# A gated attention and SwiGLU kernel: five instead of six work pairs at the head of a run, and a place for VectorE's small steps before the products

## The chip, the cores and the metric

The kernel runs on one core of a Trainium2 chip. The metric is the time of one execution on the device in microseconds; several executions are timed, and their median is given. A smaller number is better. A profile of one more execution shows what each engine did: TensorE (PE; its weight loads are listed apart as PEld), VectorE (DVE), ScalarE (ACT), GpSimd (POOL), and the DMA queue of SyncE (SP).

## The reference

With S = 2048 rows, D = 512 and F = 1792, one input x goes through two branches, which a gate mixes row by row:

```python
g = sigmoid((x * gate_w).sum(-1, keepdims=True))
qkv = x @ wqkv                          # 32 heads of 16
p = softmax(q @ k.T * 16 ** -0.5)       # per head, 2048 x 2048
a = concat(p @ v) @ wo
b = (silu(x @ w1) * (x @ w3)) @ w2
out = g * a + (1 - g) * b
```

## The kernel before

Attention's scores are taken two heads at a time. Queries come in halves of 1024, so there are 2 halves x 16 pairs of heads = 32 steps, and a step has 16 blocks of 128 keys x 2 groups of 512 queries = 32 units; 1024 units in all. A unit is one **score**, `score` (L882): two matmuls (L888), one for each head of the pair, into one of two score buffers `S` in PSUM, and one exponential by ScalarE over 128 x 1024 (L892) into a buffer p (or v). Because there are two buffers `S`, a score needs the exponential of the score before the last to be over. The **product with V**, `pv` (L871), takes two units at a time and adds into the one bank `acc` (L875); after the last key block `evac` (L853) copies `acc` out (L857) and stores it.

All other matmuls, that is the projections of v, q and k that are still missing, the gate and up projections of the second branch, its second projection, and the output projection, are cut into blocks of 9 to 14 matmul pairs, which `blocks` (L767) lists in a fixed order. `feed` (L823) issues one **work pair**: one matmul on the upper 64 rows of the array and one on the lower 64, of two different blocks. When a block is through on one half, VectorE writes a small `tick` (L847), and the block goes on in the other half of the array; when it is through on both, its `done` is called, which empties the bank with VectorE. Three banks `f` serve the blocks; a bank or a second half is taken up again only some slots later (REST, GAP), so that VectorE has time.

The order of all of it is a string written out by hand, one letter for each action: Q is a score, F is a work pair, P is a product of two units. `run(n)` is a run of n scores: two scores, then work pairs, then a score and three work pairs repeated, a last score, and n/2 products. A double period `two` has eight scores and 15 work pairs, and its products in two groups. The string first has 4 runs of eight, then 15 times a run of twelve and two of ten ("thirds", 32 scores), then the LONG runs of eight, then the SHORT double periods.

A loop walks through the string. At each score it also issues what has come due: the loads of the next step's q and k (`load_step`, at a fixed score of each step), the splits of new weights on GpSimd, and the **small steps** of VectorE. These belong to the gate projection: when a gate block is done, its exponential (L494) is put into `soon` and issued behind the last score ahead of the products, and ten steps go into `small`: one addition (L495), eight reciprocals of 64 columns each (L497), and the multiplication by the up projection (L515) with the store of the result. One step is issued at a score, two where more than six are waiting. Once the last up block is done, `hurry` is set; from then on up to three steps are issued at a score.

Of the kernel before, what the change touches and what calls it, by code (L numbers as in the profile page):

```python
# [17 lines left out]
P = 128  # L18
S = 2048
D = 512  # L20
F = 1792
# [13 lines left out]
def gated_mix_kernel(ctx: ExitStack, tc: tile.TileContext, x, wqkv, wo, w1, w3, w2, gate_w, out):  # L35
# [272 lines left out]
    def load_step(s):  # L308
        half, j = divmod(s, NPAIR)
        load_q(j, half, s % 2)  # L310
        load_k(j, s % 2)
        load_guard(j, half, s % 2)
# [124 lines left out]
    small = nc.values_load(flag, min_val=0, max_val=1)  # L437
# [15 lines left out]
    soon, later, small, stages, loads = [], [], [], [], []  # L453
    hurry = False
# [186 lines left out]
    def divide(k, half):  # L641

        yield from reciprocals(k, half)
        for b in (2 * half, 2 * half + 1):
            for _ in range(5):
                yield
            if half == 0 and k < 3:
                o, r = slot("hx", F32), slot("gw", F32)
            else:
                both = wvp.tile([P, 2, 512], F32, name="v2")  # L650
                o, r = both[:, 0, :], both[:, 1, :]
            fetch_o(k, b, o, r)
            for _ in range(7):
                yield
            nc.gpsimd.tensor_mul(o, o, r)
            for _ in range(3):
                yield
            nc.sync.dma_start(N_d[P * k:P * k + P, 512 * b:512 * b + 512], o)
            yield
# [71 lines left out]
    def six_heads():  # L731

        k, rr = ND - 1, slice(0, 6 * DH)
        rows = lambda d: d[8 * k:8 * k + 6, 1024:2048].rearrange("h (a t) -> h a t", a=16)
        nc.sync.dma_start(dd[rr], rows(D_d))
        for _ in range(5):
            yield
        nc.vector.reciprocal(dd[rr], dd[rr])
        yield
        nc.sync.dma_start(rows(R_d), dd[rr])  # L740
        both = wvp.tile([P, 2, 512], F32, name="v2")
        pairs = [(both[:, 0, :], both[:, 1, :]), (slot("fr", F32), slot("sg", F32))]
        for b in (2, 3):
            o, r = pairs[b - 2]
            nc.sync.dma_start(o[rr], O_d[P * k:P * k + 6 * DH, 512 * b:512 * b + 512])
            src = R_d[8 * k:8 * k + 6, 512 * b:512 * b + 512]
            nc.sync.dma_start(r[rr], bass.AP(tensor=src.tensor, offset=src.offset, ap=[[S, 6], [0, DH], [1, 512]]))
        for _ in range(6):
            yield
        for b in (2, 3):  # L750
            o, r = pairs[b - 2]
            nc.gpsimd.tensor_mul(o[rr], o[rr], r[rr])
            split(Oh[k][rr, b - 2, :], Ol[k][rr, b - 2, :], o[rr])
            yield
# [68 lines left out]
    def feed(rest=REST, gap=GAP):  # L823
        nonlocal fed
        fed += 1
        did = 0
        for lane in range(2):
            if lanes[lane] is None:
                lanes[lane] = pick(lane, rest, gap)
        for lane in range(2):  # L830
            t = lanes[lane]
            if t is None:
                continue
            product, done, length = t["block"]
            did += 1
            second = t["turn"] is not None
            ins = product(t["ps"], slice(64 * lane, 64 * lane + 64), t["n"], second)
            if second and t["n"] == 0:
                after(ins, t["turn"])
            t["n"] += 1  # L840
            if t["n"] == length:
                lanes[lane] = None
                if second or t["alone"]:
                    done(t["ps"])
                    over[t["id"]] = clock
                else:
                    turn = nc.vector.memset(tick[:, 0:1], 0.0)  # L847
                    after(turn, ins)
                    t.update(n=0, turn=turn, since=clock)
                    ready[1 - lane].append(t)  # L850
        return did

    def evac(j, half):  # L853
        if half == 1 and j == NPAIR - 1:
            return
        u = wk.tile([P, 512], F32, name="u")
        nc.vector.tensor_copy(u, acc)  # L857
        for gq in range(2):
            t = 1024 * half + 512 * gq
            for h in range(2):  # L860
                r = 32 * (2 * gq + h)
                hh = 2 * j + h
                nc.sync.dma_start(D_d[hh:hh + 1, t:t + 512], u[r + DH:r + DH + 1, :])
        for gq in range(2):
            t = 1024 * half + 512 * gq
            for h in range(2):
                r = 32 * (2 * gq + h)
                hh = 2 * j + h
                nc.sync.dma_start(O_d[DH * hh:DH * hh + DH, t:t + 512], u[r:r + DH, :])

    def pv(two):  # L871
        for j, half, k, gq, n, p in two:
            for h in range(2):
                r = 32 * (2 * gq + h)
                nc.tensor.matmul(acc[r:r + DH + 1, :], V[:, k, 2 * j + h, :], p[:, h, :],  # L875
                                 start=k == 0, stop=k == NT - 1)
            if type(n) is int or issued < 32 * THIRDS:
                free.append(n)
        if k == NT - 1:
            evac(j, half)  # L880

    def score(j, half, k, gq):  # L882
        i = (NPAIR * half + j) % 2
        ps = psum2()
        t = 512 * gq
        for h in range(2):
            r = 64 * h
            nc.tensor.matmul(ps[:, h, :], Kt[i][r:r + 50, P * k:P * k + P],  # L888
                             Qt[i][r:r + 50, t:t + 512], start=True, stop=True)
        n = free.pop(0)  # L890
        p = (wk if type(n) is int else wvp).tile([P, 2, 512], F32, name=f"p{n}" if type(n) is int else n)
        nc.scalar.activation(p, ps, AF.Exp, scale=SCALE)  # L892
        return j, half, k, gq, n, p
# [3 lines left out]


    NP = 8
    THIRDS, LONG, SHORT = 16, 35, 28  # L900
    run = lambda n, m=6: "QQ" + "F" * m + "QFFF" * (n - 3) + "Q" + "P" * (n // 2)
    two = "QFFF" * 5 + "QPPQQPP"
    order = run(8) * 4 + (run(12) + run(10) * 2) * (THIRDS - 1) + run(8) * LONG + "QQ" + "F" * 7 + two * SHORT + "QFFF" * 5 + "QPPPP"
    MORE = ["v0", "v1", "v2", "v3"]
    free = list(range(NP))

# [2 lines left out]
    for i, c in enumerate(order):  # L909
        clock += 1 if c != "P" else 4  # L910
        if c == "Q":
            step = issued // 32 + 1
            if issued % 32 == (22 if 128 <= issued < 160 else 14 if issued < 640 else 21 if issued < 672 else 6) and step < 2 * NPAIR:
                assert NQK - qk_left >= (NQK if step >= NPAIR else 8 * min(step // 4, ND - 1))
                load_step(step)
            pend.append(score(*next(units)))
            issued += 1
            while splits and splits[0][0] <= issued:
                splits.pop(0)[1]()
            while soon and order[i + 1] == "P":  # L920
                soon.pop(0)()
            if issued % 128 == (40 if issued // 128 == 5 else 12) and 1 <= issued // 128 < 8:
                stages.append(divide((issued // 128 - 1) % 4, (issued // 128 - 1) // 4))
            if issued == 64 * NPAIR - 22:
                stages.append(six_heads())
            if small or later and hurry:
                for _ in range(3 if hurry else 1 + (len(small) > (6 if len(over) < FIRST - 16 else 0))):
                    if small or later and hurry:
                        (small or later).pop(0)()
            if loads and (hurry or issued % 2 or len(over) > FIRST - 12):  # L930
                loads.pop(0)()
            for stage in stages[:1]:
                if next(stage, stages) is stages:
                    stages.pop(0)
        elif c == "F":
            feed()
        else:
            pv(pend[:2])
            pend = pend[2:]
            if issued == 32 and not pend:  # L940
                free += MORE
# [92 lines left out]
```

## Time and profile before

| | before |
|---|---|
| median of 3 runs | 1396.81 us (1395.8 to 1397.53) |
| profiled execution, its own time | 1396.22 us |
| its span, first to last instruction | 1394.4 us |
| TensorE busy | 1386.5 us (99%) |
| ScalarE busy | 1025.1 us (74%) |
| VectorE busy | 491.5 us (35%) |
| GpSimd busy | 335.8 us (24%) |
| granted TensorE clock | 1.0 |

A row of the timeline gives the start in us from the span's start, the length in us, the engine, the line of the kernel, the operation, the tiles out<-in, the shape, and how many instructions are merged (x). In square brackets stands how long the engine stood idle before it, and what released it. A score is two matmuls on different rows of the array, which start together; so are the two of a work pair. A row of the waits has the waiting engine, tile and line, what it waited for, and then the sum in us, the number of waits and the longest. In the costliest groups of the page stand busy us, mean ns of one, and after the second bar the idle time before them with its releaser.

### The profile page before, as it was taken

How to read it: one execution, taken by the hardware profiler on the slowest of the kernel's cores; microseconds unless marked ns; L12 is line 12 of the kernel's file. 1: busy time of each engine (PE TensorE's matmuls, PEld its weight loads, DVE VectorE, ACT ScalarE, POOL GpSimd, SP SyncE). 2: the span in 40 equal slices, each digit the busy share in tenths (PEclk: the TensorE clock that was granted, in tenths of full speed). 3: DMA queues.
4: the chain of work that ended last, by engine and by line, in shares of the span. 5: the costliest groups of instructions: out<-in, count | busy, mean ns of one | idle time of the engine just before them, and what ended most of it. 6: DMA issues, size and time to landing. Idle time of an engine off the chain costs nothing.

```text
span 1394.4 us, 29335 instructions
## 1 busy us (share of the span) xinstructions
PE 1386.5 (99%) x11601; PEld 836.8 (60%) x11601; DVE 491.5 (35%) x1101; ACT 1025.1 (74%) x1151; POOL 335.8 (24%) x371
## 2 busy tenths in 40 slices
PE   9999999999999999999999999999999999999998
PEld 8766565656566565656565566566566555555554
DVE  6411111446464646564555545431111110110113
ACT  5467677777778677778777777777677787887884
POOL 6104344210111011101110114543253431232402
PEclk9999999999999999999999999999999999999999
DMA  9505455532323233332233424536534554444632
GB/s 272 139 10 144 98 145 142 120 94 62 77 71 91 60 80 78 76 86 71 62 78 77 107 67 108 122 107 124 110 105 91 118 123 88 96 100 98 162 110 84
DMA packets 111186, 141.30 MB, mean 101 GB/s; under 512 B 16422, under 2 KB 69414, under 8 KB 108066
## 3 DMA queue, kind: packets, MB, share of 16 engines
q1 hardware_dynamic: 109888, 137.40, 40.7%
q8 instruction: 93, 1.52, 0.5%
q10 hardware_dynamic: 1154, 1.97, 0.4%
q14 instruction: 51, 0.42, 0.1%
HBM read 90.69 MB, written 48.61 MB: 100 GB/s over the span
## 4 chain that ended last, share of the span: by engine, by line
PE 95%; DVE 1%; issue 0%; DVEq 0%
PE acc L875 33%; PE f L460 27%; PE S L888 19%; PE f L584 11%; PE f L674 2%; PE f L760 1%; PE f L681 1%; DVE xH L686 0%; DVE xL L686 0%; PE f L960 0%; DVE sg L497 0%; PE S L960 0%; DVE u L949 0%; DVE sg L515 0%; PE S L971 0%
## 5 line engine op out<-in xcount | busy, mean ns | idle before, releaser
L892 ACT ACTIVATE p<-S 128x1024 f32<-128x1024 f32 x864 | 817.2, 1027 | 273.6 <-PE S L888 272.2
L888 PE MATMUL S<-Qt,Kt 50*128 50x512 f32 x2048 | 409.9, 407 | 1.2 <-SPq L316 1.1
L875 PE MATMUL acc<-p,V 128*17 128x512 f32 x3456 | 400.8, 594 | 0.0
L888 PEld LDWEIGHTS S<-Qt,Kt 50*128 50x128 f32 x2048 | 187.8, 184 | 153.7 <-issue 73.0
L875 PEld LDWEIGHTS acc<-p,V 128*17 128x17 f32 x3456 | 88.7, 97 | 235.8 <-issue 235.1
L497 DVE RECIPROCAL sg<-sg 128x64 f32<-128x64 f32 x448 | 209.6, 518 | 52.6 <-issue 48.6
L460 PE MATMUL f<-xH,fl 64*128 64x512 f32 x1104 | 223.8, 394 | 0.1
L460 PE MATMUL f<-xH,fh 64*128 64x512 f32 x1104 | 221.6, 389 | 0.0
L460 PE MATMUL f<-xL,fh 64*128 64x512 f32 x1104 | 221.2, 389 | 0.0
L892 ACT ACTIVATE v<-S 128x1024 f32<-128x1024 f32 x160 | 153.0, 1027 | 54.7 <-PE S L888 54.4
L460 PEld LDWEIGHTS f<-xH,fh 64*128 64x128 f32 x1104 | 108.6, 184 | 23.3 <-DVE tick L847 0.2
L460 PEld LDWEIGHTS f<-xL,fh 64*128 64x128 f32 x1104 | 109.1, 187 | 22.4
L351 POOL CAST fh<-fr 128x512 fp32r<-128x512 f32 x35 | 22.1, 631 | 416.7 <-DMA fr<-in_B_w_dram 368.1
L460 PEld LDWEIGHTS f<-xH,fl 64*128 64x128 f32 x1104 | 108.8, 186 | 22.2 <-DVE raw L511 0.5
L847 DVE MEMSET tick<- 1x1 f32 x205 | 12.1, 59 | 310.4 <-PE f L584 152.5
L875 PE MATMUL acc<-v,V 128*17 128x512 f32 x640 | 77.1, 593 | 0.0
L584 PE MATMUL f<-xL,fh 64*128 64x512 f32 x208 | 66.2, 390 | 0.0
L584 PE MATMUL f<-xH,fl 64*128 64x512 f32 x208 | 65.9, 390 | 0.0
L584 PE MATMUL f<-xH,fh 64*128 64x512 f32 x208 | 61.2, 390 | 0.0
L857 DVE COPY u<-acc 128x512 f32<-128x512 f32 x31 | 21.5, 692 | 102.3 <-PE acc L875 102.3
L489 DVE COPY gs<-f 128x512 f32<-128x512 f32 x56 | 38.4, 687 | 53.2 <-PE f L460 52.4
L495 DVE TENSOR_SCALAR sg<-sg 128x512 f32<-128x512 f32 x56 | 26.1, 466 | 88.1 <-ACT sg L494 84.8
(221 smaller groups left out, 1417.2 us busy)
## 6 DMA issues: line engine op xcount, KB each, us to landing
Kt<-kH_d SPq DMA_DIRECT2D x124, 128.0 KB
h_d<-sg SPq DMA_DIRECT2D x56, 256.0 KB
sg<-h_d SPq DMA_DIRECT2D x43, 256.0 KB
fr<-in_B_w_dram SPq DMA_DIRECT2D x42, 256.0 KB
Qt<-qH_d SPq DMA_DIRECT2D x128, 64.0 KB
Kt<-kL_d SPq DMA_DIRECT2D x62, 128.0 KB
Qt<-qL_d SPq DMA_DIRECT2D x64, 64.0 KB
b_d<-yy SPq DMA_DIRECT2D x16, 256.0 KB
```

Of the source, the lines that this page charges most:

```text
L351: nc.gpsimd.tensor_copy(hi, src)
L460: return nc.tensor.matmul(ps, w[i == 1][r, k, :], (xL if i == 2 else xH)[b][r, k, :], start=n == 0 and not second, stop=n == 3 * ND - 1 an ...
L489: nc.vector.tensor_copy(gs, ps)
L495: small.append(lambda: nc.vector.tensor_scalar(sg, sg, 1.0, None, op0=OP.add))
L497: small.append(lambda q=q: nc.vector.reciprocal(sg[:, q:q + 64], sg[:, q:q + 64]))
L584: ins = nc.tensor.matmul(ps, hs[t][q][i == 1][r, P * o:P * o + P], (w2L if i == 2 else w2H)[q][r, o, :], start=n == 0 and not second, stop ...
L674: return nc.tensor.matmul(ps, ot[t][i == 1][r, P * k:P * k + P], wo_[k][i == 2][r, :], start=n == 0 and not second, stop=n == 3 * ND - 1 a ...
L681: return nc.tensor.matmul(ps, o_rows(t, k, i == 1)[r, :], wo_[k][i == 2][r, :], start=n == 0 and not second, stop=n == LATE - 1 and (secon ...
L857: nc.vector.tensor_copy(u, acc)
L875: nc.tensor.matmul(acc[r:r + DH + 1, :], V[:, k, 2 * j + h, :], p[:, h, :], start=k == 0, stop=k == NT - 1)
L888: nc.tensor.matmul(ps[:, h, :], Kt[i][r:r + 50, P * k:P * k + P], Qt[i][r:r + 50, t:t + 512], start=True, stop=True)
L892: nc.scalar.activation(p, ps, AF.Exp, scale=SCALE)
```

## The change

At the head of a run, behind its first two scores, stand five work pairs instead of six; only the four runs at the very beginning keep six. The string has 51 instead of 35 runs of eight behind the thirds, and 12 instead of 28 double periods. Beside that, ahead of the first product of each group, up to two of VectorE's waiting small steps are issued, as long as `hurry` is not set.

```diff
     NP = 8
-    THIRDS, LONG, SHORT = 16, 35, 28
-    run = lambda n, m=6: "QQ" + "F" * m + "QFFF" * (n - 3) + "Q" + "P" * (n // 2)
+    THIRDS, LONG, SHORT = 16, 51, 12
+    run = lambda n, m=5: "QQ" + "F" * m + "QFFF" * (n - 3) + "Q" + "P" * (n // 2)
     two = "QFFF" * 5 + "QPPQQPP"
-    order = run(8) * 4 + (run(12) + run(10) * 2) * (THIRDS - 1) + run(8) * LONG + "QQ" + "F" * 7 + two * SHORT + "QFFF" * 5 + "QPPPP"
+    order = run(8, 6) * 4 + (run(12) + run(10) * 2) * (THIRDS - 1) + run(8) * LONG + "QQ" + "F" * 7 + two * SHORT + "QFFF" * 5 + "QPPPP"
...
         elif c == "F":
             feed()
         else:
+            if order[i - 1] != "P" and not hurry:
+                for _ in range(2):
+                    if small:
+                        small.pop(0)()
             pv(pend[:2])
             pend = pend[2:]
```

## The prediction, made before the changed kernel ran

> **What bounds the kernel now.** I read the page first, then the order of time around one run in the middle, then the waits of the weight loads, then the first and last starts of each kind of period.
>
> ```profile
> span 1394.4 us, 29335 instructions
> PE 1386.5 (99%) x11601; PEld 836.8 (60%) x11601; DVE 491.5 (35%) x1101; ACT 1025.1 (74%) x1151; POOL 335.8 (24%) x371
> PE 95%; DVE 1%; issue 0%; DVEq 0%
> L892 ACT ACTIVATE p<-S 128x1024 f32<-128x1024 f32 x864 | 817.2, 1027 | 273.6 <-PE S L888 272.2
> ```
>
> TensorE is busy 99% of the span and is 95% of the chain that ended last, so the time is what the order string asks of TensorE, plus what TensorE waits. The share hides the second part: a busy matmul may be one that waits. ScalarE's exponentials are the candidate, because inside a run they follow each other without a gap. The timeline of one run of eight scores (the first row holds its first two scores; columns: start, length, engine, line, operation):
>
> ```profile
> 801.24 0.74 PE L888 MATMUL S<-Qt,Kt 50*128 50x512 f32 x4
> 801.84 1.03 ACT L892 ACTIVATE p<-S 128x1024 f32<-128x1024 f32 x1 [2.32 <-PE S L888]
> 802.98 0.19 PEld L888 LDWEIGHTS S<-Qt,Kt 50*128 50x128 f32 x2
> 803.20 0.40 PE L888 MATMUL S<-Qt,Kt 50*128 50x512 f32 x2
> 803.44 0.40 PE L460 MATMUL f<-xH,fl 64*128 64x512 f32 x2
> 807.84 0.39 PE L888 MATMUL S<-Qt,Kt 50*128 50x512 f32 x2
> 808.16 0.62 PE L875 MATMUL acc<-p,V 128*17 128x512 f32 x4
> 811.72 0.73 PE L888 MATMUL S<-Qt,Kt 50*128 50x512 f32 x4
> ```
>
> The period is 811.72 − 801.24 = 10.48 us. From the third score (803.20) to the eighth (807.84) stand five groups of a score and three work pairs, 20 slots in 4.64 us: **0.232 us a slot**. The third score reuses the buffer of the first, whose exponential ends at 801.84 + 1.03 = 802.87. The score's weight load starts 0.11 us after that, its matmul 0.33 us after. That is the margin the change spends.
>
> **What the exchange is worth without waits.** Both order strings count to 1024 scores, 2566 work pairs (F) and 512 products with V. 16 double periods become 16 more runs of eight; 45 runs of ten and twelve and 51 runs of eight carry one pair fewer than they would under the old rule, 96 in all, which pays for the 16 × 6 pairs by which an old run exceeds a double period. The starts of the regions:
>
> ```profile
> 102.54 0.73 PE L888 MATMUL S<-Qt,Kt 50*128 50x512 f32 x4
> 144.83 0.73 PE L888 MATMUL S<-Qt,Kt 50*128 50x512 f32 x4
> 738.08 0.74 PE L888 MATMUL S<-Qt,Kt 50*128 50x512 f32 x4
> 1095.40 0.73 PE L888 MATMUL S<-Qt,Kt 50*128 50x512 f32 x4
> 1114.87 0.73 PE L888 MATMUL S<-Qt,Kt 50*128 50x512 f32 x4
> 1359.68 0.73 PE L888 MATMUL S<-Qt,Kt 50*128 50x512 f32 x4
> ```
>
> 26 double periods take 1359.68 − 1114.87, 9.416 each. A run of eight costs 10.48 − 9.416 = 1.064 more for six pairs more, which at 0.232 are 1.39: a double period loses 0.33 us more at its extra switch between scores and products. Exchange: 16 × 1.064 = +17.0. Pairs left out: 96 × 0.232 = −22.3. Sum **−5.3 us**, if every pair left out shortens its run by a whole slot.
>
> **Does it? The third score then waits.** With five pairs the third score is wanted at 803.20 − 0.23 = 802.97, 0.10 us after the first exponential's end, and its weight load would start 0.12 us before that end. The trace has this situation where ScalarE was once late by itself:
>
> ```profile
> 642.78 1.03 ACT L892 ACTIVATE p<-S 128x1024 f32<-128x1024 f32 x1 [0.20 <-ACT v L892]
> 643.63 0.40 PE L460 MATMUL f<-xH,fh 64*128 64x512 f32 x2
> 643.86 0.19 PEld L888 LDWEIGHTS S<-Qt,Kt 50*128 50x128 f32 x2 [0.26 <-ACT p L892]
> 643.87 0.49 PE L888 MATMUL S<-Qt,Kt 50*128 50x512 f32 x2
> 644.20 0.39 PE L460 MATMUL f<-xH,fl 64*128 64x512 f32 x2
> 644.78 0.19 PEld L888 LDWEIGHTS S<-Qt,Kt 50*128 50x128 f32 x2 [0.16 <-ACT p L892]
> 648.97 0.62 PE L875 MATMUL acc<-v,V 128*17 128x512 f32 x4
> PEld S L888 <- ACT p L892: 49.8, 65, 0.9
> ```
>
> The exponential ends at 643.81; it is the weight load, not the matmul, that waits for it, and it starts 0.05 us later. The score's matmul is recorded at 643.87 but lasts 0.49 instead of 0.39, so it really began 0.10 later; its next pair at 644.20 says the same: 644.20 − 0.23 = 643.97, **0.16 us after the exponential's end**. That pair follows the last one by 644.20 − 643.63 = 0.57, against 0.46 for two slots. The waits view counts 65 such waits. So the new third score comes at 0.16 instead of 0.10: a stall of 0.05 to 0.06 a run. I take 0.055 (bounds 0.03 and 0.08, the rows being rounded to 0.01): 96 × 0.055 = **+5.3 us**, all of the gain.
>
> In the first run of each 32 scores the first exponential starts later:
>
> ```profile
> 780.01 0.73 PE L888 MATMUL S<-Qt,Kt 50*128 50x512 f32 x4
> 780.64 1.03 ACT L892 ACTIVATE p<-S 128x1024 f32<-128x1024 f32 x1 [2.45 <-PE S L888]
> ```
>
> 0.63 after the score against 0.60: 0.03 more in 15 runs of twelve and a fourth of 51, 28 runs: **+0.8**.
>
> **The pace behind it.** From then on each score's weight load waits, as at 644.78. From the pair behind that first late score to the products it takes 648.97 − 644.20 = 4.77, against 808.16 − 803.44 = 4.72 in the free run, over the same six scores: up to +0.05. A shorter stretch of the kind:
>
> ```profile
> 795.40 0.19 PEld L888 LDWEIGHTS S<-Qt,Kt 50*128 50x128 f32 x2 [0.27 <-ACT p L892]
> 795.73 0.39 PE L460 MATMUL f<-xH,fl 64*128 64x512 f32 x2
> 797.68 3.20 PE L875 MATMUL acc<-p,V 128*17 128x512 f32 x28
> ```
>
> 1.95 from the pair behind a late score to the products, two scores between; in the free run 4.72 less three groups of 0.928 is 1.94, so +0.01. I take 0.03 for a run of eight, 0.04 for ten, 0.05 for twelve, as the gaps are five, seven and nine: 51 × 0.03 + 30 × 0.04 + 15 × 0.05 = **+3.5** (bounds 0 and 6).
>
> **VectorE's small steps.** Excess over the plain periods: (1095.40 − 738.08) − 34 × 10.48 = 1.0 in the long runs; 738.08 − 102.54 = 635.5 against 15 × (144.83 − 102.54) = 634.4, 1.2 in the thirds. 2.2 us in all is what late VectorE work and late ScalarE starts cost there today. An example of the former:
>
> ```profile
> 486.21 0.39 PE L888 MATMUL S<-Qt,Kt 50*128 50x512 f32 x2
> 486.54 1.43 DVE L497 RECIPROCAL sg<-sg 128x64 f32<-128x64 f32 x3
> 487.44 0.06 DVE L847 MEMSET tick<- 1x1 f32 x1
> 487.49 0.40 PE L888 MATMUL S<-Qt,Kt 50*128 50x512 f32 x2
> 788.84 0.43 DVE L495 TENSOR_SCALAR sg<-sg 128x512 f32<-128x512 f32 x1 [2.02 <-ACT sg L494]
> 789.29 1.79 DVE L497 RECIPROCAL sg<-sg 128x64 f32<-128x64 f32 x4
> ACT p L892 <- ACT p L892: 0.7, 4, 0.2
> ```
>
> Reciprocals stand in front of what the next pair waits for, and the score comes after 1.28 instead of 0.93. The added pops take up to two of the ten steps of a gate block out of that stretch and put them before the products, where VectorE waits anyway. The late ScalarE starts (four at 0.2 in the last row, two or so more in the runs that write other buffers, as the one at 642.78) cost 0.10 each today (0.57 against 0.46 above), 0.6 in all; of the 1.6 left I credit VectorE's relief with half, **−0.8** (bounds −1.6 and +1.6, as the pattern of pairs against runs shifts). What the new place adds: the first popped step can wait for the gate's exponential, and the copy of the sums and the next ticks queue behind it; the run that began at 780.01 ends a period later, near 790.5, so that wait ended 1.7 us before the next run, and the copy behind it cannot start before the last product anyway: nothing, while the exponential comes no later than that. The late ScalarE starts meet no margin any more and cost all of their 0.2: six times 0.10, **+0.6**.
>
> **What moves beside it.** The gate blocks end, by the letters, after 668 scores instead of 643, so the loads for the second projection move past the request for step 21 (after 661 scores) and before that for step 22 (after 678).
>
> ```profile
> 921.08 12.31 SPq L546 DMA_DIRECT2D sg<-h_d  x6
> 933.96 0.42 SPq L300 DMA_DIRECT2D Qt<-qH_d  x1
> ```
>
> Today step 21's loads stand behind a block of 12.3 us; step 22's would then, and it is wanted 26 scores or some 34 us later. Nothing, unless the block grows to 34 us; then a wait of PE for Qt shows.
>
> **Sum**: −5.3 + 5.3 + 0.8 + 3.5 − 0.8 + 0.6 = +4.1. The profiled execution took 1396.2 us (span 1394.4, 1.8 around it), 0.6 under the median of the three. 1396.2 + 4.1 gives **1400.3**. Own range: stalls ±2.4, pace −3.5 to +2.5, VectorE −0.8 to +2.4; taken together 1396 to 1405.
>
> **Rivals.**
> 1. *The wait doesn't reach the third score* (the other side, faster). If the load of the weights may wait elsewhere and only the matmul needs the exponential, the gate lies at 0.05 after its end and the score is wanted at 0.10: no stall, no slower pace. −5.3 − 0.8 = −6: 1390. It decides at 0.10 us. Against it: the load itself waits at 643.86 and 644.78. In part (half the stall, no loss of pace) 1393. Chance 0.17. The Trainium skill, "TensorE: Matmul & The Clock Gate", the table at its head, says that TensorE's queue pulls weight loads ahead of matmuls in flight; by that rule alone the load would be out of the way and the time 1390, but a load that waits for a semaphore is not covered by it, and the 65 waits above speak against it.
> 2. *Stall as worked out, pace kept, VectorE relieved*: −5.3 + 5.3 + 0.8 − 0.8 = 0, 1396 to 1399. For it: the +0.01 over two scores. Chance 0.30.
> 3. *The stall is larger than the analog shows*: the left-out pair saves nothing, since the scores' pace is the exponentials' pace. +17: 1413; with a stall of 0.12 instead of 0.055, 1406. Against it: the pair at 644.20 stood 0.16 behind the exponential's end less one slot, after a longer wait than the one expected here. Chance 0.08.
> 4. My sum: 0.45.
>
> 0.2% of the median is 2.8 us, about what a measurement here can tell: 1394.0 to 1399.6 is "same". Case 1 is faster. Case 2, and the low end of case 4 (0.02 to 0.05 of it), are same; some of case 2 may fall to faster (0.02). Faster 0.19, same 0.30, slower 0.51. The range reaches down to 1392.0, which leaves out the full form of case 1 (0.1), and up to 1405.0, which leaves out case 3.
>
> **What would show it.** Right: the weight load of the third score in nearly every run has "ACT p" as its releaser, the waits view counts hundreds instead of 65, third score 1.78 us after the run's first instead of 1.96; period of eight 10.33 to 10.36 instead of 10.25; ScalarE without a gap through each run. The number of switches falls from 141 to 125 groups of products, and double periods keep 9.41. Wrong: a period of 10.25 (rival 1) or 10.48 (rival 3); the excess in the gate phase far from 1 to 2 us; a wait of PE for Qt or Kt around scores 672 to 704.

## The result, and the profile after

The changed kernel takes 1403.05 us (median of five runs, 1402.47 to 1403.47) against 1396.74 for the kernel before: 1.0045 times as long, 95% interval 1.0034 to 1.0057. The forecast was 1400.3, slower. The profiled execution took 1402.54 us, 6.3 more than that of before.

The page of the changed kernel (span, engines, chain by engine):

```profile
span 1400.8 us, 29332 instructions
PE 1391.9 (99%) x11601; PEld 818.5 (58%) x11601; DVE 493.4 (35%) x1101; ACT 1014.9 (72%) x1151; POOL 335.9 (24%) x371
PE 94%; DVE 0%; DMA 0%; SPq 0%; POOL 0%; issue 0%; ACT 0%; DVEq 0%; POOLq 0%
```

The page hardly differs: TensorE is as "busy" as before, 99%. What it now waits for does not show in its share, since a matmul that waits for its weights is recorded as running (the one at 807.65 below lasts 0.45 instead of 0.40). One run of eight in the timeline of the changed kernel shows it. The first row holds the first two scores; the exponentials stand there twice, the first one alone and all eight of the run in one row, as the view shows no gap between them:

```profile
805.92 0.74 PE L888 MATMUL S<-Qt,Kt 50*128 50x512 f32 x4
806.52 1.03 ACT L892 ACTIVATE p<-S 128x1024 f32<-128x1024 f32 x1 [1.88 <-PE S L888]
806.52 7.44 ACT L892 ACTIVATE p<-S 128x1024 f32<-128x1024 f32 x8 [1.88 <-PE S L888]
807.60 0.19 PEld L888 LDWEIGHTS S<-Qt,Kt 50*128 50x128 f32 x2 [0.22 <-ACT p L892]
807.65 0.45 PE L888 MATMUL S<-Qt,Kt 50*128 50x512 f32 x2
807.94 0.40 PE L460 MATMUL f<-xL,fh 64*128 64x512 f32 x2
808.18 0.19 PEld L460 LDWEIGHTS f<-xH,fl 64*128 64x128 f32 x2
808.41 0.40 PE L460 MATMUL f<-xH,fl 64*128 64x512 f32 x2
808.51 0.19 PEld L888 LDWEIGHTS S<-Qt,Kt 50*128 50x128 f32 x2
808.64 0.40 PE L888 MATMUL S<-Qt,Kt 50*128 50x512 f32 x2
812.71 3.63 PE L875 MATMUL acc<-p,V 128*17 128x512 f32 x32
816.26 0.73 PE L888 MATMUL S<-Qt,Kt 50*128 50x512 f32 x4
```

The first exponential ends at 806.52 + 1.03 = 807.55. The third score's weight load, which follows five pairs now, starts at 807.60, 0.05 after it, and waited 0.22 for it. The next pair stands at 807.94, so that the score really began at 807.71, 0.16 after the exponential's end. The period is 816.26 − 805.92 = 10.34: of the 0.23 that a pair is worth, 0.14 is gained and 0.09 lost. It is so everywhere: in the trace of the changed kernel the third score's load starts 0.05 us after the end of the first exponential in each of the 96 runs with five pairs, and of all 1024 scores 641 have a load that starts within 0.06 us after the end of the exponential that it needs; in the trace of before there are 60.

The starts of the regions after; and in the second block one more start of before. The rows at 1262.62 and at 1256.04 are score 920. Behind the two scores of that row the changed string has seven work pairs and the old one two products; from there on both have the same 12 double periods and the same end:

```profile
103.02 0.73 PE L888 MATMUL S<-Qt,Kt 50*128 50x512 f32 x4
733.37 0.73 PE L888 MATMUL S<-Qt,Kt 50*128 50x512 f32 x4
1262.62 0.73 PE L888 MATMUL S<-Qt,Kt 50*128 50x512 f32 x4
1271.62 0.74 PE L888 MATMUL S<-Qt,Kt 50*128 50x512 f32 x4
1375.29 0.73 PE L888 MATMUL S<-Qt,Kt 50*128 50x512 f32 x4
```

```profile
1256.04 0.74 PE L888 MATMUL S<-Qt,Kt 50*128 50x512 f32 x4
```

| stretch | before | after | difference |
|---|---|---|---|
| up to the thirds | 102.54 | 103.02 | +0.5 |
| thirds, 45 runs | 635.54 | 630.35 | −5.2 |
| from there to score 920 | 517.96 | 529.25 | +11.3 |
| from score 920 to the end of the span | 138.36 | 138.18 | −0.2 |

The stretch up to the thirds has the same order in both kernels; it scatters by about a microsecond between executions (101.9 to 103.1 in all profiles of this study). Eleven double periods after take 1375.29 − 1271.62, 9.42 each, as before. The waits of the weight loads in the changed kernel:

```profile
PEld S L888 <- ACT p L892: 46.2, 149, 0.9
PEld S L888 <- ACT v L892: 4.5, 20, 0.5
```

169 waits, against 65 + 4 before. The view does not count every late load: the one at 808.51 started 0.14 after the load before it had ended (808.18 + 0.19) and has no bracket, while the idle times that are shown with one are longer.

One wait was not forecast. The run that starts at 930.44 takes 941.64 − 930.44 = 11.20, 0.85 more than its neighbours:

```profile
923.77 0.38 SPq L300 DMA_DIRECT2D Qt<-qH_d  x1
929.96 0.39 SPq L546 DMA_DIRECT2D fr<-h_d  x1
935.17 0.61 POOL L547 CAST fh<-fr 128x512 fp32r<-128x512 f32 x1 [14.45 <-DMA fr<-h_d]
935.86 1.28 POOL L548 TENSOR_TENSOR fl<-fr,fh 128x512 fp32r<-128x512 f32 x1
937.19 0.49 PE L584 MATMUL f<-xH,fl 64*128 64x512 f32 x1 [0.58 <-POOL fl L548]
```

Step 21's loads begin at 923.77 in SyncE's queue; the load of a piece of h, which a block of the second projection needs, stands behind them and is issued at 929.96. GpSimd stood 14.45 us for it, and a work pair waited for `fl`, the second of the two parts into which GpSimd splits that piece.

### The profile page after: what moved, and what is told of

Same layout as the page of the kernel before. It is cut to its first block, busy times and chain, and to the rows that moved or that the text cites. A ratio compares the mean times of both kernels' runs of the same rounds, so it can differ in the third digit from the quotient of the medians.

```text
span 1400.8 us, 29332 instructions
## 1 busy us (share of the span) xinstructions
PE 1391.9 (99%) x11601; PEld 818.5 (58%) x11601; DVE 493.4 (35%) x1101; ACT 1014.9 (72%) x1151; POOL 335.9 (24%) x371
## 4 chain that ended last, share of the span: by engine, by line
PE 94%; DVE 0%; DMA 0%; SPq 0%; POOL 0%; issue 0%; ACT 0%; DVEq 0%; POOLq 0%
PE acc L875 32%; PE f L460 27%; PE S L888 19%; PE f L584 11%; PE f L674 2%; PE f L760 1%; PE f L681 1%; DMA fr<-h_d 0%; DVE xH L686 0%; SPq L293 0%; DVE xL L686 0%; PE f L964 0%; POOL fl L548 0%; SPq L300 0%; ACT v L892 0%
## 5 line engine op out<-in xcount | busy, mean ns | idle before, releaser
L888 PEld LDWEIGHTS S<-Qt,Kt 50*128 50x128 f32 x2048 | 184.5, 184 | 191.2 <-issue 86.9
L497 DVE RECIPROCAL sg<-sg 128x64 f32<-128x64 f32 x448 | 206.0, 514 | 34.1 <-issue 30.1
L584 PE MATMUL f<-xH,raw 64*128 64x512 f32 x192 | 54.9, 392 | 0.0
```

Source lines behind the costliest of these rows:

```text
L497: small.append(lambda q=q: nc.vector.reciprocal(sg[:, q:q + 64], sg[:, q:q + 64]))
L584: ins = nc.tensor.matmul(ps, hs[t][q][i == 1][r, P * o:P * o + P], (w2L if i == 2 else w2H)[q][r, o, :], start=n == 0 and not second, stop ...
```

## The experiments

The theories: **A**, the third score's weight load waits for the first exponential, and this takes the gain of the exchange. **B**, VectorE's small steps at their new place cost the time. **C**, the mix of periods costs it, wherever a pair stands. **D**, even six pairs leave too little margin. All diffs are against the kernel that the text names.

### The order string alone

Against the changed kernel:

```diff
-            if order[i - 1] != "P" and not hurry:
-                for _ in range(2):
-                    if small:
-                        small.pop(0)()
```

> The changed order string alone, without the small steps ahead of the products. Theory A (the third score's weight load waits for the first exponential, and that takes the gain of the exchange): nearly all of the 6.3 us of slow-down is here, 1403 us, plus the 0.8 us with which the small steps were credited as a relief: 1402.5 to 1404.5; runs of eight at 10.35 us, the third weight load 0.05 us after the end of the first exponential in every run. Theory B (the small steps at their new place hold VectorE up and cost the time): 1396 to 1399, with runs of eight near 10.25.

Measured: 1404.78 us (1402.39 to 1405.40), 1.0053 times before (1.0039 to 1.0066), 0.3 above the upper end of the forecast. Starts of the long runs and of the region behind them, the longest wait, and the load and the split of the piece of h that it is for:

```profile
732.94 0.73 PE L888 MATMUL S<-Qt,Kt 50*128 50x512 f32 x4
1264.93 0.73 PE L888 MATMUL S<-Qt,Kt 50*128 50x512 f32 x4
937.83 0.50 PE L584 MATMUL f<-xH,fl 64*128 64x512 f32 x1 [2.03 <-POOL fl L548]
929.99 2.20 SPq L546 DMA_DIRECT2D fr<-h_d  x2
935.82 0.61 POOL L547 CAST fh<-fr 128x512 fp32r<-128x512 f32 x1 [15.94 <-PE f L584]
```

The slow-down is there without the small steps, so B falls. The thirds end 0.4 earlier than in the changed kernel, and 2.7 us are lost in the long runs, where the wait for the piece of h is larger (the whole run takes 4.0 more than its neighbours). The load is issued at the same time as in the changed kernel (929.99 against 929.96); GpSimd begins with the piece 0.65 later (935.82 against 935.17; the bracket there names TensorE and not the load), and TensorE's run begins 0.8 earlier (929.65 against 930.44), so that it waits longer. Whether the missing small steps do this is not shown: how far that wait differs from execution to execution was not measured, and the run times scatter by 3 us. Elsewhere the small steps change little here.

### The small steps alone

Against the kernel before, the same four lines are added and the order string is left.

> The kernel before with the small steps ahead of the products alone; the order string is the old one. Theory A, with the credit of the prediction: 1396.0 us, 0.8 less than before (bounds -1.6 and +1.6), the excess over the plain periods of 10.48 falls from 1.0 us in the long runs. Theory B: 1399 or more.

Measured: 1396.06 us, 0.9994 times before (0.9984 to 1.0003): 0.6 less, near the 0.8 that was forecast, but it can't be told from no difference. They do what they are for in the thirds, whose excess over their plain periods falls from 1.1 to 0.5 us. In the long runs, where the fall was forecast, the excess stays (1.2 against 1.0), because the steps cost there once (VectorE in the timeline):

```profile
862.02 1.43 DVE L495 TENSOR_SCALAR sg<-sg 128x512 f32<-128x512 f32 x1 [2.97 <-ACT sg L494]
863.49 1.38 DVE L497 RECIPROCAL sg<-sg 128x64 f32<-128x64 f32 x3
864.78 0.63 DVE L857 COPY u<-acc 128x512 f32<-128x512 f32 x1
865.32 2.25 DVE L497 RECIPROCAL sg<-sg 128x64 f32<-128x64 f32 x5
867.04 0.06 DVE L847 MEMSET tick<- 1x1 f32 x1
```

The addition waits for the gate's exponential, takes 1.43 instead of some 0.43, three reciprocals and the copy of the sums stand behind it and five more reciprocals behind that, and the tick that a pair waits for comes so late that this run loses 0.91. It is the mishap that the prediction priced at nothing "while the exponential comes no later than that".

### The sixth pair at the end of the run instead of its head

Against the kernel before; the numbers of long and double periods stay:

```diff
-    run = lambda n, m=6: "QQ" + "F" * m + "QFFF" * (n - 3) + "Q" + "P" * (n // 2)
+    run = lambda n, m=6: "QQ" + "F" * 5 + "QFFF" * (n - 4) + "QFFFF" + "Q" + "P" * (n // 2)
-    order = run(8) * 4 + ...
+    first = "QQ" + "F" * 6 + "QFFF" * 5 + "Q" + "PPPP"
+    order = first * 4 + ...
```

> The kernel before with all its counts (35 long runs, 28 double periods, 2566 pairs), but the sixth pair of each run moved from its head to the place before its last score; the four first runs keep it at the head. Theory A: the third score waits as in the changed kernel, and the pair is then paid in full: a run of eight takes 10.35 + 0.23 = 10.58 instead of 10.48, a run of ten 13.30 instead of 13.19, of twelve 16.07 instead of 15.91; 35 x 0.10 + 30 x 0.11 + 15 x 0.16 = +9.2 us, 1406. Theory C (what counts is the mix of long and double periods, the place of a pair does not): 1396 to 1398.

Measured: 1404.50 us, 1.0057 times before (1.0043 to 1.0070): 7.9 us more, with nothing changed but the place of one pair in each run.

```profile
743.00 0.74 PE L888 MATMUL S<-Qt,Kt 50*128 50x512 f32 x4
1113.85 0.73 PE L888 MATMUL S<-Qt,Kt 50*128 50x512 f32 x4
```

35 runs of eight take 370.85, 10.60 each (10.58 forecast, 10.51 before). The total is 1.5 under the 1406 that was forecast, but C would have 1396 to 1398: the place of the pair counts.

### Seven pairs at the head

Against the kernel before:

```diff
-    THIRDS, LONG, SHORT = 16, 35, 28
+    THIRDS, LONG, SHORT = 16, 30, 33
-    ... run(8) * LONG ...
+    ... run(8, 7) * LONG ...
```

> The kernel before with seven pairs instead of six at the head of the long runs, and 30 long and 33 double periods, so that scores and pairs come out the same. Theory A: with six pairs the third score waits for nothing, so the seventh only costs its slot: 30 x 0.232 - 5 x 1.064 = +1.6 us, 1398.4, less up to 0.5 where late exponentials now meet more margin; run of eight 10.71. Theory D (the margin at six is too small already, so each pair more at the head gains): 1396 or less, run of eight under 10.65.

Measured: 1399.38 us, 1.0022 times before (1.0013 to 1.0031).

```profile
737.80 0.73 PE L888 MATMUL S<-Qt,Kt 50*128 50x512 f32 x4
1061.47 0.73 PE L888 MATMUL S<-Qt,Kt 50*128 50x512 f32 x4
913.26 0.50 PE L584 MATMUL f<-xH,raw 64*128 64x512 f32 x1 [1.06 <-DVE tick L847]
```

30 runs take 323.67, 10.79 each; a plain one 10.71 to 10.72, as forecast. Behind the 1.0 us over the forecast stands above all a new collision, at 913.26, where a pair waits 1.06 us for a tick of VectorE behind six reciprocals and the run loses 1.6 in all. D falls: the seventh pair costs its slot. With five on one side and seven on the other, six is the cheapest of the three that were run.

### Halved exponentials, in both kernels

```diff
-        nc.scalar.activation(p, ps, AF.Exp, scale=SCALE)
+        nc.scalar.activation(p[:, :, 0:256], ps[:, :, 0:256], AF.Exp, scale=SCALE)
...
-                nc.tensor.matmul(acc[r:r + DH + 1, :], V[:, k, 2 * j + h, :], p[:, h, :],
+                nc.tensor.matmul(acc[r:r + DH + 1, :].rearrange("p (a t) -> p a t", a=2), V[:, k, 2 * j + h, :],
+                                 p[:, h, 0:256][:, None, :].to_broadcast([P, 2, 256]),
```

> The kernel before with exponentials over half the columns: ScalarE takes 256 of each 512 columns, and the products read these twice. It leaves out half of the exponentials, so its output isn't the reference's; TensorE's matmuls keep their number and size. Theory A: the old string has no wait for the exponentials to lose but the late starts, so it gains 1 to 2 us at most: 1395 to 1396.5; exponentials near 0.6 us instead of 1.03.

> The changed kernel with the same halved exponentials, which leave out half of that work. Theory A: no third score waits any more, a run of eight takes 10.48 - 0.23 = 10.25, and the exchange pays its -5.3 us against the kernel before with halved exponentials, less 0.9 for the wait of the pieces of h that the changed kernel shows near 936 us: 4 to 5 us under that kernel, 1390.5 to 1392. Theory B or C (VectorE, or the mix of periods, makes the change slow): 4 us or more over that kernel, 1400 or more.

Both runs leave out half of the exponentials. Measured on the same chip: 1395.43 us with the old string, as forecast (0.9991 times before, 0.9982 to 1.0000), **1392.01** with the changed one (0.9967, 0.9955 to 0.9979). The changed string is now 3.4 us the faster of the two, where it was 6.3 the slower. A run of eight of the changed string, its first two exponentials, the bounds of the long runs, and two waits:

```profile
798.93 0.73 PE L888 MATMUL S<-Qt,Kt 50*128 50x512 f32 x4
799.53 1.09 ACT L892 ACTIVATE p<-S 128x512 f32<-128x512 f32 x2 [2.35 <-PE S L888]
800.67 0.39 PE L888 MATMUL S<-Qt,Kt 50*128 50x512 f32 x2
809.18 0.73 PE L888 MATMUL S<-Qt,Kt 50*128 50x512 f32 x4
727.15 0.73 PE L888 MATMUL S<-Qt,Kt 50*128 50x512 f32 x4
1251.82 0.73 PE L888 MATMUL S<-Qt,Kt 50*128 50x512 f32 x4
PEld S L888 <- ACT p L892: 10.2, 12, 0.9
PEld f L584 <- POOL fl L548: 2.0, 1, 2.0
```

809.18 − 798.93 = 10.25, the 10.48 − 0.23 of the exchange to the hundredth, and the 149 waits for exponentials are 12. The third score comes 1.74 after the run's first, where the changed kernel has 807.71 − 805.92 = 1.79. The forecast of 4 to 5 us was missed by 0.6, because the wait for the piece of h was larger here, 2.0 us; the 51 runs take 524.67, 10.288 each, 1.8 more in all than 51 plain ones of 10.253. Without that wait, taken from the one execution that was profiled, the exchange gave 5.2 (5.3 forecast).

### Step 21's loads earlier

Against the changed kernel:

```diff
-            if issued % 32 == (22 if 128 <= issued < 160 else 14 if issued < 640 else 21 if issued < 672 else 6) and step < 2 * NPAIR:
+            if issued % 32 == (22 if 128 <= issued < 160 else 14 if issued < 640 else 12 if issued < 672 else 6) and step < 2 * NPAIR:
```

> The changed kernel with the loads for step 21 issued after 652 scores instead of 661. Theory: the wait of 0.85 us that the changed kernel has at the sixth score of the run at 930 us (a pair waits for GpSimd's half of a piece of h, whose load stood in SyncE's queue behind the 13 loads of step 21) goes away: 1402.2, 0.9 less than the changed kernel's 1403.05, and the run takes 10.35 instead of 11.20. Rival: the load of the piece is late for another reason (its store, or GpSimd): no change, 1403.

Measured: 1401.69 us (1401.51 to 1402.09), 1.0037 times before (1.0023 to 1.0051), 1.4 under the changed kernel's median.

```profile
923.60 0.38 SPq L546 DMA_DIRECT2D fr<-h_d  x1
936.18 0.39 PE L584 MATMUL f<-xH,fl 64*128 64x512 f32 x1
930.19 0.73 PE L888 MATMUL S<-Qt,Kt 50*128 50x512 f32 x4
940.52 0.74 PE L888 MATMUL S<-Qt,Kt 50*128 50x512 f32 x4
```

The piece of h is asked for at 923.60 instead of 929.96, the pair waits for nothing, and the run takes 10.33. The wait was the queue's order, and it cost about a microsecond of the 6.3: 0.87 in this run, 1.4 between the medians. (The long runs together are only 0.4 shorter in the profile, as others among them took a little longer than in the changed kernel.)

### The pair taken from the end of the run

Against the kernel of the last section:

```diff
-    run = lambda n, m=5: "QQ" + "F" * m + "QFFF" * (n - 3) + "Q" + "P" * (n // 2)
+    run = lambda n: "QQ" + "F" * 6 + "QFFF" * (n - 4) + "QFF" + "Q" + "P" * (n // 2)
-    order = run(8, 6) * 4 + ...
+    order = ("QQ" + "F" * 6 + "QFFF" * 5 + "Q" + "PPPP") * 4 + ...
```

> The changed kernel with step 21's loads after 652 scores, and with the left-out pair taken from the end of the run (two pairs ahead of the last score) instead of its head, where six stand again; all counts as in the changed kernel. Theory A with a stall and a pace of its own: only the last score's weight load waits, 0.055 to 0.065 us a run, and nothing is left behind it to run slower: runs of eight 10.31, ten 13.02, twelve 15.74; against the kernel before 16 x 1.064 - 96 x 0.168 = +0.9 us, 1397.5, 4 us under the changed kernel with step 21's loads moved. Rival (the run's exponentials as a whole set its length, wherever the pair is taken): 10.35 as in the changed kernel, 1401.5.

Measured: 1397.55 us (1396.31 to 1398.41), 1.0008 times before (0.9999 to 1.0018), 4.1 under the same kernel with the pair taken from the head.

```profile
802.56 0.73 PE L888 MATMUL S<-Qt,Kt 50*128 50x512 f32 x4
808.88 0.19 PEld L888 LDWEIGHTS S<-Qt,Kt 50*128 50x128 f32 x2 [0.23 <-ACT p L892]
812.87 0.73 PE L888 MATMUL S<-Qt,Kt 50*128 50x512 f32 x4
```

812.87 − 802.56 = 10.31 as forecast: only the last weight load waits, once. So the stall of a gated score and the slower pace behind it are two costs; the second, some 0.04 us in a run of eight, falls away where no score stands behind.

### The small steps up to 600 scores only

Against the kernel with the small steps alone:

```diff
-            if order[i - 1] != "P" and not hurry:
+            if order[i - 1] != "P" and issued < 600:
```

> The kernel before with the small steps ahead of the products, but only up to 600 scores; what this is for is a version under both kernels. In the run with the small steps alone the excess of the runs of twelve fell from 0.80 to 0.17 us, and one run at 864 us lost 0.91 where VectorE's addition stood ahead of the copy of the sums. Without that: 1395.7, 0.9 under before (bounds 1395.2 and 1396.6).

Measured: 1395.31 us (1394.69 to 1396.01), 0.9993 times before (0.9984 to 1.0002).

```profile
863.56 0.69 DVE L857 COPY u<-acc 128x512 f32<-128x512 f32 x1 [0.71 <-PE acc L875]
865.88 0.06 DVE L847 MEMSET tick<- 1x1 f32 x1
```

Against the starts of their runs (863.4 here, 863.8 there) the copy and the tick come 0.8 us sooner than in the rows at 864.78 and 867.04. It is the lowest median among the kernels here that leave nothing out, 1.1 us under before's; by the interval it cannot be told from no change.

## Why the prediction was right

The direction, the range and the mechanism held; the size was 4.1 us for 6.3. By its steps:

- **The exchange without waits, −5.3.** Right: −5.2 in the halved kernels once the wait for h is taken off, and 10.25 for the run of eight.
- **The third score's stall, 0.055.** Right at its place: load 0.05, score 0.16 after the exponential's end. The analog in the trace of before, one score that ScalarE had delayed by chance, gave it before the change was ever run. That the pair's place is what counts, and not how many there are, the run with the sixth pair at the end shows by itself (+7.9 us).
- **The pace behind it, 0.03 to 0.05 a run.** Right that it exists, as the pair taken from the end shows; with the later first exponentials it came out somewhat small. The five-pair run of eight takes 10.35 in the middle (forecast 10.33 to 10.36), but a run of ten 13.08, 0.12 over its 13.19 − 0.23 (0.095 forecast), and one of twelve 15.84, 0.16 over (0.135). With 51 × 0.105 for the runs of eight this is 11.4 us in all, where stall, later starts and pace were summed to 9.6. This is the term that was mis-sized: 1.8 of the 2.2 that are missing. The next two points go in opposite directions and nearly cancel, which is luck; the 0.5 before the thirds is scatter.
- **"What moves beside it" cost nothing, it said; it cost about one microsecond.** This step failed. The direction in which the loads pass each other was right, but the prediction looked at step 22's request behind the pieces, and not at the pieces behind step 21's request. The pieces of h have no 26 scores of lead.
- **VectorE, −0.8, and late ScalarE starts, +0.6.** The excess of 2.2 us over the plain periods fell to about 0.7 besides the wait for h, which is more than was credited. It was not the small steps: the order string alone, without them, has about 0.7 besides that wait too. What in the new string did it was not tested. Alone on the old string the steps gave 0.6, inside its interval of no change.
- **Rival 1** (the wait misses the third score, 1390) needs the load not to wait; it does, 0.05 us past the exponential's end in each of the 96 runs. Its time is what the changed string reaches when the exponentials are short: 1392.0. The rule that the Trainium skill states in "TensorE: Matmul & The Clock Gate", at the table of its head, is not contradicted: the weight load at 808.51 did run while the pair at 808.41 was in flight, but the one at 807.60 had a semaphore of ScalarE to wait for. **Rival 2** left out the slower pace and the wait for h. **Rival 3** (nothing saved) is out: the runs did become 0.07 (twelve) to 0.13 (eight) shorter.
- That the waits view would count hundreds was wrong in its number, 169, as it leaves out loads that are only a little late; by the starts of the loads it is 641.

## What to carry to other kernels

Where two engines run at nearly the same pace (0.928 us of matmuls for a score and its three pairs, against (7.44 − 1.03) / 7 = 0.92 from one exponential to the next here), a slot taken out of one's stretch is paid only up to the margin that it has at that place, so price it at the first wait behind it and not by the slot. Look for one instance in the trace where the wait happened by chance: it shows which instruction waits, and its price. If a slot must go, take it where nothing of the stretch stands behind it.

## What the runs showed of the hardware that was not expected

A weight load that waits for a semaphore costs less than its delay. A free load stands 0.22 before its score, as at 802.98 and 803.20 in the run of before. In the changed kernel the score recorded at 807.65 would have had its load at 807.43; the load at 807.60 was late by 0.17, and its score by 0.06; the load at 808.51 stands 0.10 behind the pair at 808.41 that it would else start with, and its score at 808.64 follows that pair by the usual 0.23. About a tenth of a microsecond of a late weight load is nearly free, and only what goes beyond it is seen. All scores of the changed kernel that stand between two work pairs say the same: where the load starts 0.02 to 0.12 us behind the pair before the score (some 400 scores), the next pair comes 0.003 to 0.009 later than in a free run; at 0.18 it is 0.05, at 0.20 it is 0.08. These few thousandths are the slower pace behind the first stall: a run whose scores all wait for exponentials is only some 0.01 us a score slower than a free one. Why they are not nothing was not found.
